# Second expert layer with relu outputs as stationary operand, 256 rows per expert, and a changed order of gathers and table loads

## The chip, the cores and the metric

The kernel runs on one core of a Trainium2 chip. The time of a run is the device time of that core in microseconds; the kernel before was timed three times. One further execution was recorded by the hardware profiler, and all rows shown come from it. Differences of about 0.5% are the least that a measurement of this kernel can tell.

## The reference, cut to what matters

Three stages follow one another: an attention block with heads mixed before and after the softmax, a gated dense feed-forward block, and a mixture of eight experts in which each token goes to one expert. Only the last is changed:

```python
# x: (1792, 768), the dense block's output; w1: (8, 768, 1024); w2: (8, 1024, 768)
logits = x @ w_gate
expert_idx = np.argmax(logits, axis=1)
gate_w = softmax(logits)[np.arange(N), expert_idx]
for e in range(8):
    mask = expert_idx == e
    h = np.maximum(x[mask] @ w1[e], 0.0)
    out[mask] = gate_w[mask, None] * (h @ w2[e])
```

With the reference's inputs the eight experts get 259, 213, 241, 186, 222, 236, 225 and 210 tokens.

## The kernel before, in words

All is written in `feed_forward` (line 415) with an order of instructions fixed by hand: each engine and SP, which issues the loads, executes its instructions in the order in which the program writes them.

**Precision by three products.** Every operand of a large matmul is split into a rounded high part in a reduced float32 type and the low part that is left. `mm3` (line 472) adds three matmuls: high weight by high data (L473), low weight by high data (L474), high weight by low data (L475). The weight tile is the stationary operand, 128 by 128; the data streams past it, 448 columns in the dense layers (the 1792 tokens in four parts `u`) and `CAP` = 264 columns in the experts.

**Weights.** A list `src` names all weight tiles in order: 72 uses for the dense layers (k = 0 to 71), then for each expert four tiles of w1 and four of w2 (k = 72 to 135), 768 KB each. `take` (line 463) hands out the next and looks ahead: it loads up to i+3 on SP (L438, buffer `wraw`, three of them), splits i+2 and loads i+4. `split` (line 440) casts the high part on ScalarE (`whi`, L447) and subtracts for the low part (`wlo`, L451) on GpSimd, or on VectorE where k is in `LOW_W` (line 46: every third k).

**Routing.** `route(u)` (line 577) is a generator in four pieces: the one-hot choice `oh`; slots by prefix sums on TensorE; the list of tokens of the first expert (L609, L610, table `TB0`); then the gate weights and four scatters on GpSimd's queue of (token, gate) pairs into a DRAM table `tab` (L628). The tokens themselves are turned into rows (`turn_row`, `take_row`, `put_row`) and stored in DRAM as `x2`. For the last part, u = 3, this stands between the dense layers and the experts, with `warm` matmuls on constants in between (lines 768 to 796). Then three loads on SP fetch the table for all experts into `TB` (L793); they wait for all table scatters. TB holds 88 rows by 3 per expert.

**Experts.** `fetch(e)` (line 635) issues three indirect loads of 88 rows each from `x2` on GpSimd's queue (L640). `gather(e)` (line 643) transposes them on TensorE (L648; per piece of 128 features three transposes of 88 rows), ScalarE casts the high part (`xhi`), VectorE subtracts the low (`xlo`). The loop at line 831 runs for each expert eight groups `f` of the first layer, 18 matmuls each, with relu on ScalarE (`hhi`) and the low part on VectorE (`hlo`), into PSUM tiles `mm` of which there are five. After group 3 (5 for expert 0) it calls `fetch(e + 1)`. The second layer computes six groups `c` of 24 matmuls, 128 output features by 264 tokens, with the w2 tile stationary; ScalarE copies each group out of PSUM (L864), and after some of them pieces of `gather(e + 1)` run on TensorE (`GATHER`, two after each of the first two groups, one after each of the next two). The result has features on partitions, so `put` (line 799) transposes it back on TensorE (L807, six pieces of three), scales by the gate on VectorE or ScalarE (L814, L812) and scatters three times 88 rows to the output (L816). Three of its pieces run in the second layer (`PARTS`), three in the next expert's first layer.

**Behind the experts.** `blocks` (line 820) counts how many blocks of 128 tokens overflow `CAP`; `overflow` (line 872) computes these in a loop. With at most 264 tokens per expert it does not run.

## Time and profile before

| | |
|---|---|
| three runs | 1424.41, 1429.89, 1430.99 us; median 1429.89 |
| profiled execution, its own time | 1431.59 us |
| its span | 1429.7 us |
| TensorE (PE) busy | 1357.1 us, 95% |
| TensorE weight loads (PEld) | 1179.4 us, 82% |
| VectorE (DVE), ScalarE (ACT), GpSimd (POOL) busy | 57%, 48%, 45% |
| mean granted TensorE clock | 0.981 of 2.4 GHz |
| from HBM, to HBM | 222.46 MB, 45.94 MB |

Attention and the dense layers take the first 1056 us or so, the experts run from 1078 us. Matmuls are pipelined: the duration shown of one is longer than the distance from its start to the next one's, and only the distances add up to time. A wait row says who waited, what came last, the total, how often and the longest.

### The profile page before, as it was taken

How to read it: one execution, taken by the hardware profiler on the slowest of the kernel's cores; microseconds unless marked ns; L12 is line 12 of the kernel's file. 1: busy time of each engine (PE TensorE's matmuls, PEld its weight loads, DVE VectorE, ACT ScalarE, POOL GpSimd, SP SyncE). 2: the span in 40 equal slices, each digit the busy share in tenths (PEclk: the TensorE clock that was granted, in tenths of full speed). 3: DMA queues.
4: the chain of work that ended last, by engine and by line, in shares of the span. 5: the costliest groups of instructions: out<-in, count | busy, mean ns of one | idle time of the engine just before them, and what ended most of it. 6: DMA issues, size and time to landing. Idle time of an engine off the chain costs nothing.

```text
span 1429.7 us, 24918 instructions
## 1 busy us (share of the span) xinstructions
PE 1357.1 (95%) x9144; PEld 1179.4 (82%) x9144; DVE 810.1 (57%) x1562; ACT 690.2 (48%) x1325; POOL 636.4 (45%) x589
## 2 busy tenths in 40 slices
PE   8999999999999999999999999999997899999995
PEld 3677776776777789999999999999977899999995
DVE  3677777766767746606991798189623232433331
ACT  4676666766665533434333433344223354454441
POOL 4676567557654454441112112211035366665662
PEclk9999999999999999999999999999998899999998
DMA  7887787787787687686647765776523466656550
GB/s 243 243 259 236 224 261 243 225 256 245 217 250 213 208 276 269 232 317 214 238 178 263 247 216 188 255 250 213 194 87 125 137 196 205 206 194 203 171 197 21
DMA packets 117060, 307.88 MB, mean 215 GB/s; under 512 B 29198, under 2 KB 72302, under 8 KB 116817
## 3 DMA queue, kind: packets, MB, share of 16 engines
q1 hardware_dynamic: 112577, 294.17, 63.5%
q0 software_dynamic: 4352, 12.02, 3.0%
q8 instruction: 75, 1.23, 0.4%
q14 instruction: 56, 0.46, 0.1%
HBM read 222.46 MB, written 45.94 MB: 188 GB/s over the span
## 4 chain that ended last, share of the span: by engine, by line
PE 74%; DMA 10%; issue 5%; POOL 5%; ACT 2%; SPq 2%; DVE 1%; POOLq 0%; ACTq 0%; DVEq 0%
PE mm L473 16%; PE mm L475 16%; PE mm L474 16%; PE pso L274 8%; PE psm L246 7%; PE psv L302 4%; PE psq L233 4%; DMA qraw<-in_qt 2%; DMA row<-x,TB 2%; POOL wlo L451 2%; DMA xm<-S 2%; DMA wraw<-in_w 2%; POOL row L640 1%; SPq L241 1%; PE tp L648 1%
## 5 line engine op out<-in xcount | busy, mean ns | idle before, releaser
L473 PE MATMUL mm<-xhi,whi 128*128 128x448 f32 (+1 forms) x960 | 326.8, 340 | 1.4 <-ACT xhi L492 1.4
L475 PE MATMUL mm<-xlo,whi 128*128 128x448 f32 (+1 forms) x960 | 322.6, 336 | 0.9 <-POOL xlo L493 0.9
L474 PE MATMUL mm<-xhi,wlo 128*128 128x448 f32 (+1 forms) x960 | 321.8, 335 | 0.0
L451 POOL TENSOR_TENSOR wlo<-wraw,whi 128x1536 fp32r<-128x1536 f32 x54 | 189.3, 3508 | 135.8 <-ACT whi L447 135.0
L474 PE MATMUL mm<-hhi,wlo 128*128 128x264 f32 (+1 forms) x672 | 216.9, 323 | 4.3 <-POOL wlo L451 4.3
L473 PE MATMUL mm<-hhi,whi 128*128 128x264 f32 (+1 forms) x672 | 220.5, 328 | 0.0
L475 PE MATMUL mm<-hlo,whi 128*128 128x264 f32 (+1 forms) x672 | 216.4, 322 | 0.0
L274 PEld LDWEIGHTS pso<-kk,e 120*112 120x112 f32 x1440 | 170.8, 177 | 49.7 <-POOL kk L266 14.8
L447 ACT CAST whi<-wraw 128x1536 fp32r<-128x1536 f32 x136 | 200.9, 1478 | 8.0 <-DMA wraw<-in_w 7.1
L681 DVE RECIPROCAL e<-e 128x448 f32<-128x448 f32 x48 | 141.7, 2952 | 97.8 <-ACT e L680 97.8
L274 PE MATMUL pso<-kk,e 120*112 120x120 f32 x1440 | 180.6, 268 | 16.5 <-ACT AT L282 6.8
L475 PEld LDWEIGHTS mm<-xlo,whi 128*128 128x128 f32 x960 | 181.8, 189 | 13.1 <-POOL xlo L493 2.4
L473 PEld LDWEIGHTS mm<-xhi,whi 128*128 128x128 f32 x960 | 182.0, 190 | 12.1 <-ACT xhi L492 1.7
L474 PEld LDWEIGHTS mm<-xhi,wlo 128*128 128x128 f32 x960 | 182.1, 190 | 10.1
L689 POOL TENSOR_TENSOR hlo<-e,hhi 128x448 fp32r<-128x448 f32 x48 | 57.2, 1191 | 292.5 <-ACT hhi L688 292.5
L246 PE MATMUL psm<-xm,K 120*120 120x448 f32 x360 | 169.8, 554 | 5.6 <-DMA xm<-S 5.4
L266 POOL TENSOR_SCALAR kk<-K,r 120x120 f32<-120x120 f32 x180 | 108.5, 603 | 144.2 <-DVE r L263 114.2
L254 ACT ACTIVATE e<-psm,nm 120x448 f32<-120x448 f32 x180 | 115.5, 642 | 96.1 <-DVE r L263 94.3
L474 PEld LDWEIGHTS mm<-hhi,wlo 128*128 128x128 f32 x672 | 128.5, 191 | 10.2 <-POOL wlo L451 5.0
L473 PEld LDWEIGHTS mm<-hhi,whi 128*128 128x128 f32 x672 | 128.6, 191 | 5.0
L475 PEld LDWEIGHTS mm<-hlo,whi 128*128 128x128 f32 x672 | 128.4, 191 | 5.3
L688 ACT CAST hhi<-e 128x448 fp32r<-128x448 f32 x48 | 27.3, 568 | 213.9 <-DVE e L683 213.9
(127 smaller groups left out, 2082.7 us busy)
## 6 DMA issues: line engine op xcount, KB each, us to landing
wraw<-wf SPq DMA_DIRECT2D x72, 768.0 KB
wraw<-in_w SPq DMA_DIRECT2D x64, 768.0 KB
wlo<-wl SPq DMA_DIRECT2D x54, 768.0 KB
xm<-S SPq DMA_DIRECT2D x360, 105.0 KB
f<-in_wx SPq DMA_DIRECT2D x72, 384.0 KB
wf<-cva SPq DMA_DIRECT2D x72, 192.0 KB
wl<-wlo SPq DMA_DIRECT2D x18, 768.0 KB
qraw<-in_qt SPq DMA_DIRECT2D x56, 180.0 KB
```

The source lines that it names most:

```text
L233: nc.tensor.matmul(ps[:m, :S], QS[t, h // 3][i][:, h % 3, :m], k, start=(i == 0), stop=(i == 1))
L246: nc.tensor.matmul(ps[:, :S], K1, XS.pop(n), start=True, stop=True)
L254: nc.scalar.activation(e, ps[:, :S], AF.Exp, bias=nm, scale=1.0, accum_out=su)
L266: nc.gpsimd.tensor_scalar(out=kk, in0=K2, scalar1=r2, scalar2=1.0, op0=ALU.mult, op1=ALU.mult)
L274: nc.tensor.matmul(po[:, c, :120], e[:, 112 * c:112 * c + 112], kk, start=True, stop=True)
L447: A.copy(a, r)
L451: (V if k in LOW_W else G).tensor_tensor(out=b, in0=r, in1=a.bitcast(F32), op=ALU.subtract)
L473: nc.tensor.matmul(ps, w[0][:, j, :], x[0], start=first, stop=False)
L474: nc.tensor.matmul(ps, w[1][:, j, :], x[0], start=False, stop=False)
L475: nc.tensor.matmul(ps, w[0][:, j, :], x[1], start=False, stop=last)
L681: V.reciprocal(out=e, in_=e)
L689: G.tensor_tensor(out=hl, in0=e, in1=hh.bitcast(F32), op=ALU.subtract)
```

## The change

For experts 1 to 7 the second layer is turned round: the relu outputs (128 hidden features by 128 tokens) become the stationary operand and w2, stored with hidden features on partitions and all 768 outputs in the free dimension, streams past them in halves of 384 columns. The four sums (two halves of tokens by two halves of outputs) are held in four PSUM tiles through all eight hidden groups and come out as token rows, so that one scaling copy each (ScalarE for the first half of the outputs, VectorE for the second) and two scatters of 128 rows finish the expert. These experts hold 256 tokens in two tiles of 128; expert 0 keeps 264 tokens in three of 88 and the old second layer. `fetch(e + 1)` follows the first group in place of the fourth (expert 0: still the sixth); one gather piece follows each hidden group but the first. The table is loaded by five loads after the third group of expert 0; the rest of `route(3)` stands ahead of `warm(6)` and `gather(0)`; all four last row halves are turned in one go, two of them through `mm` buffers. From k = 72 on every second `wlo` goes to VectorE.

```diff
-CAP = 264
-TS = CAP // 3
+CAP = [264] + [256] * 7
+TS = CAP[0] // 3
...
-LOW_W = {0} | {k for k in range(200) if k % 3 == 2 and not 18 < k < 72}
+LOW_W = {0} | {k for k in range(200) if (k % 3 == 2 and k < 18) or (k % 2 == 0 and k >= 72)}
...
         def fetch(e):
             RG[e] = []
-            for t in range(3):
-                r = ro.tile([112, DM], F32, name="row")
+            n = 128 if e else TS
+            for t in range(2 if e else 3):
+                r = ro.tile([128, DM], F32, name="row")
...
         def gather(e):
             XE[e] = []
+            n = 128 if e else TS
             for c in range(6):
...
-                for t in range(3):
-                    nc.tensor.transpose(p[:, t * TS:t * TS + TS], RG[e][t][:TS, 128 * c:128 * c + 128], ID[:TS, :TS])
+                for t, r in enumerate(RG[e]):
+                    nc.tensor.transpose(p[:, t * n:t * n + n], r[:n, 128 * c:128 * c + 128], ID[:n, :n])
...
-        for j in (0, 1):
-            turn_row(3, j, 1)
-        for j in (0, 1):
+        for j in range(4):
+            turn_row(3, j, 1, pm if j > 1 else None)
+        for j in range(4):
             take_row(3, j, 1)
             put_row(3, j, 384, DM)
-        warm(1)
         next(go)
-        for j in (2, 3):
-            turn_row(3, j, 1)
-        for j in (2, 3):
-            take_row(3, j, 1)
-            put_row(3, j, 384, DM)
-        warm(2)
+        warm(3)
         next(go)
         fetch(0)
+        for _ in go:
+            pass
         warm(6)
         for _ in gather(0):
             pass
-        for _ in go:
-            pass
-        for t in range(3):
-            ld = nc.sync.dma_start(out=TB[:, :, t, :], in_=tab.rearrange("(e s) t -> s e t", e=NE)[t * TS:t * TS + TS])
...
+        def put(e, acc):
+            for t in range(2):
+                row = RT[:, (2 * e + 1 + t) % NE, :]
+                g = TB[:, e, t, 1:2].bitcast(F32)
+                A.activation(row[:, :384], acc[t][0][:, :384], AF.Copy, scale=g)
+                V.tensor_scalar(out=row[:, 384:], in0=acc[t][1][:, :384], scalar1=g, scalar2=None, op0=ALU.mult)
+                sc = G.indirect_dma_start(out=out, out_offset=bass.IndirectOffsetOnAxis(ap=TB[:, e, t, 0:1], axis=0), in_=row, in_offset=None, bounds_check=NT - 1, oob_is_err=False)
+                apart("out", sc)
...
                 hs.append((hh, hl))
+                if e == 0 and f == 2:
+                    for t in range(5):
+                        o, i = (TBF[:, t, :], tab[t * TS:t * TS + TS]) if t < 3 else (TB[:, 1:, t - 3, :], tab.rearrange("(e s) t -> s e t", e=NE)[128 * (t - 3):128 * (t - 2), 1:])
+                        ld = nc.sync.dma_start(out=o, in_=i)
+                        for sc in routed:
+                            tc.add_manual_dep(from_inst=ld.ins, to_name=sc.ins.name, info=mybir.DependencyInfo(mybir.DependencyClass.Sync, mybir.DependencyReason.DATA))
+                if f == (5 if e == 0 else 0) and e + 1 < NE:
+                    fetch(e + 1)
                 next(done, None)
-                if e == 0 and f == 3:
+                if e == 0 and f == 6:
                     blocks()
-                if f == (5 if e == 0 else 3) and e + 1 < NE:
-                    fetch(e + 1)
...
+            acc = [[pm.tile([128, 512], F32, name="mm") for hf in range(2)] for t in range(2)]
+            for f in range(8):
+                if f % 2 == 0:
+                    w = [z.rearrange("p a b -> p (a b)") for z in take()]
+                for t in range(2):
+                    for hf in range(2):
+                        o = f % 2 * DM + 384 * hf
+                        h = [z[:, 128 * t:128 * t + 128] for z in hs[f]]
+                        ps = acc[t][hf][:, :384]
+                        nc.tensor.matmul(ps, h[0], w[0][:, o:o + 384], start=(f == 0), stop=False)
+                        nc.tensor.matmul(ps, h[0], w[1][:, o:o + 384], start=False, stop=False)
+                        nc.tensor.matmul(ps, h[1], w[0][:, o:o + 384], start=False, stop=(f == 7))
+                if f > 0:
+                    next(parts, None)
+            put(e, acc)
```

The weight layout on the host and the overflow loop are adapted to the new form of w2; for expert 0 the old second layer and its `put`, now `put0` with its own table `TBF`, are kept.

## Rows read from the trace of the kernel before

**Rows 1.** Stretches: us, busy (instructions) PE, PEld, DVE, ACT, POOL; PE clock; DMA share; GB/s.

```profile
1056.00:1078.12 22.12, 16.64 (x89) 10.85 (x87) 4.73 (x17) 3.46 (x9) 6.83 (x11) 0.87 0.25 69
1078.12:1097.82 19.70, 19.70 (x149) 19.70 (x148) 6.12 (x20) 6.99 (x12) 8.70 (x10) 0.89 0.34 105
1097.82:1133.48 35.66, 23.74 (x174) 22.89 (x172) 9.30 (x13) 12.06 (x21) 17.87 (x7) 0.81 0.47 143
1133.48:1411.29 277.81, 271.04 (x2251) 269.59 (x2249) 94.04 (x138) 130.31 (x202) 168.53 (x96) 0.99 0.58 184
```

**Rows 2.** The same view, experts 1 to 7 (fastest, last, sum of all seven).

```profile
1252.51:1290.97 38.46, 38.46 (x327) 38.38 (x325) 14.67 (x21) 19.28 (x31) 23.74 (x14) 1.00 0.64 205
...
1374.65:1413.53 38.88, 38.62 (x318) 37.75 (x315) 10.30 (x16) 15.43 (x24) 17.57 (x11) 1.00 0.30 100
sum 280.05, PE 273.02 PEld 270.70 DVE 95.18 ACT 131.17 POOL 168.81; mean PE 39.00 PEld 38.67 DVE 13.60 ACT 18.74 POOL 24.12
```

**Rows 3.** Timeline of TensorE, expert 4's second layer: start us, us, line, operation.

```profile
1281.37 0.28 PE L475 MATMUL mm<-hlo,whi 128*128 128x264 f32 x1
...
1283.89 0.28 PE L475 MATMUL mm<-hlo,whi 128*128 128x264 f32 x1
1284.01 0.49 PE L807 MATMUL tp<-CS,x2T 128*88 128x128 f32 x3
1284.34 0.39 PE L648 MATMUL tp<-CS,row 88*128 88x88 f32 x3
1284.52 0.37 PE L473 MATMUL mm<-hhi,whi 128*128 128x264 f32 x1
```

**Rows 4.** Timeline of TensorE in a dense layer.

```profile
900.00 0.37 PE L473 MATMUL mm<-hhi,whi 128*128 128x448 f32 x1
...
904.13 0.36 PE L475 MATMUL mm<-hlo,whi 128*128 128x448 f32 x1
```

**Rows 5.** Waits, 1055 to 1135 us: who, for what, us in total, times, longest.

```profile
PE tp L648 <- DMA row<-x,TB: 13.5, 6, 5.3
...
ACT whi L447 <- DMA wraw<-in_w: 6.5, 1, 6.5
```

**Rows 6.** Waits of SP's queue, 1055 to 1430 us.

```profile
SPq L793 <- DMA tab<-en,si: 25.7, 1, 25.7
```

**Rows 7.** Timeline of SP's queue, the table loads.

```profile
1089.51 1.75 SPq L793 DMA_DIRECT2D TB<-tab  x3
```

**Rows 8.** Chain of work that ended last, three links: start us, us, what.

```profile
1069.74 4.48 DMA row<-x,TB
...
1085.51 3.88 DMA tab<-en,si
...
1188.02 8.38 DMA row<-x,TB
```

**Rows 9.** Timelines of TensorE, VectorE and GpSimd at the end of the last expert.

```profile
1411.29 0.94 PE L807 MATMUL tp<-CS,x2T 128*88 128x128 f32 x6
...
1413.57 0.61 DVE L814 TENSOR_SCALAR WT<-tp,TB 88x384 f32<-88x384 f32 x1 [0.62 <-PE tp L807]
...
1415.85 0.99 POOL L816 DMA_INDIRECT out<-WT,TB  x1 [0.21 <-issue]
```

**Rows 10.** Waits of TensorE, 1133 to 1411 us.

```profile
PE tp L648 <- DMA row<-x,TB: 5.4, 5, 2.3
PE mm L474 <- POOL wlo L451: 1.4, 2, 0.7
```

**Rows 11.** VectorE's wlo subtractions: ns min/median/max from 1078; mean ns from 1133 us.

```profile
L451 DVE TENSOR_TENSOR wlo<-wraw,whi x21: 1757/1759/4934, 1081.4 to 1395.2; 128x1536 fp32r<-128x1536 f32 x21
...
L451 DVE TENSOR_TENSOR wlo<-wraw,whi 128x1536 fp32r<-128x1536 f32 x18 | 40.9, 2271 | 18.2 <-ACT whi L447 16.3 <-issue 1.9
```

**Rows 12.** Timeline of TensorE in attention, plain float32 and the next.

```profile
402.06 1.01 PE L246 MATMUL psm<-xm,K 120*120 120x448 f32 x2
402.56 0.71 PE L233 MATMUL psq<-ks,qhi 128*110 128x448 f32 x1
```

More of the change, by code (lines that the diff above doesn't have):

```diff
@@ L507, in feed_forward @@
         load(3)
-        WT = cst.tile([112, NE, DM], F32, name="WT")
+        WT = cst.tile([128, NE, DM], F32, name="WT")[:112]
         WG = cst.tile([128, 6, NE], F32, name="WG")
@@ L551, in feed_forward, with turn_row @@
         X2T, ROW, HALF, LG, routed, late = {}, {}, {}, {}, [], []
-        def turn_row(u, j, hf):
-            t = HALF[u, j, hf] = pt.tile([128, 3, 128], F32, name="tp")
+        def turn_row(u, j, hf, where=None):
+            t = HALF[u, j, hf] = where.tile([128, 512], F32, name="mm")[:, :384].rearrange("p (a b) -> p a b", b=128) if where else pt.tile([128, 3, 128], F32, name="tp")
             for i in range(3):
@@ L559, in take_row @@
             if (u, j) not in ROW:
-                ROW[u, j] = ro.tile([112, DM], F32, name="row")
-            (eng or A.copy)(ROW[u, j][:, 384 * hf:384 * hf + 384], HALF.pop((u, j, hf))[:112].rearrange("p i c -> p (i c)"))
+                ROW[u, j] = ro.tile([128, DM], F32, name="row")
+            (eng or A.copy)(ROW[u, j][:112, 384 * hf:384 * hf + 384], HALF.pop((u, j, hf))[:112].rearrange("p i c -> p (i c)"))
         def put_row(u, j, lo=0, hi=DM):
-            nc.sync.dma_start(out=x2[u * U + 112 * j:u * U + 112 * j + 112, lo:hi], in_=ROW[u, j][:, lo:hi])
+            nc.sync.dma_start(out=x2[u * U + 112 * j:u * U + 112 * j + 112, lo:hi], in_=ROW[u, j][:112, lo:hi])
         def logit(u, n):
@@ L600, in route @@
             V.tensor_reduce(out=sf, in_=sl, axis=AX.X, op=ALU.add)
-            eqs = [sm.tile([112, CAP], F16, name="at", bufs=4) for j in range(4)]
+            eqs = [sm.tile([112, CAP[0]], F16, name="at", bufs=4) for j in range(4)]
             for j in range(4):
@@ L851, in feed_forward @@
             parts = gather(e + 1) if e + 1 < NE else iter(())
[L852 to L866 removed]
+            if e == 0:
+                y = []
+                done = put0(y)
+                for c in range(6):
+                    ps = pm.tile([128, 512], F32, name="mm")[:, :CAP[0]]
+                    for f in range(8):
+                        j = c * 8 + f
+                        if j % 12 == 0:
+                            w = take()
+                        mm3(ps, w, j % 12, hs[f], f == 0, f == 7)
+                        if (c, f) in PARTS:
+                            next(done)
+                    t = yp.tile([128, U], F32, name="x2T")[:, :CAP[0]]
+                    A.copy(t, ps)
+                    y.append(t)
+                    for _ in range(GATHER[c]):
+                        next(parts, None)
+                continue
+            acc = [[pm.tile([128, 512], F32, name="mm") for hf in range(2)] for t in range(2)]
+            for f in range(8):
+                if f % 2 == 0:
[9 more added lines that the diff above has]
+                if f > 0:
                     next(parts, None)
[L868 to L869 removed]
+            put(e, acc)
 def overflow(tc, w1, w2, out, x2, tab, keep):
@@ L886, in overflow @@
                     t = rb.tile([128, 2], I32, name="ot")
-                    nc.sync.dma_start(out=t, in_=tab[bass.ds(i * 128 + (e * STR + CAP), 128), :])
+                    nc.sync.dma_start(out=t, in_=tab[bass.ds(i * 128 + (e * STR + CAP[e]), 128), :])
                     r = rb.tile([128, DM], F32, name="orow")
@@ L906, in overflow @@
                         p = pm.tile([128, 128], F32, name="om")
+                        w = wp.tile([128, 12, 128], F32, name="ow")
                         for f in range(8):
-                            j = c * 8 + f
-                            if j % 12 == 0:
-                                w = wp.tile([128, 12, 128], F32, name="ow")
-                                nc.sync.dma_start(out=w, in_=w2[e, j // 12])
-                            nc.tensor.matmul(p, w[:, j % 12, :], h[:, f, :], start=(f == 0), stop=(f == 7))
+                            i = w2[e, (c * 8 + f) // 12, :, (c * 8 + f) % 12] if e == 0 else w2[e, f // 2, :, f % 2 * 6 + c]
+                            nc.sync.dma_start(out=w[:, f, :], in_=i)
+                        for f in range(8):
+                            nc.tensor.matmul(p, w[:, f, :], h[:, f, :], start=(f == 0), stop=(f == 7))
                         y = yb.tile([128, 128], F32, name="oy")
```

61 lines of the change are left out of this document (21 added, 40 removed).

## The prediction, made before the changed kernel ran

> **What bounds the kernel now.** I first cut the span into stretches by what TensorE does [rows 1]. The experts begin at 1078.12 us and hold the last 351 us. In the first row, the hand-over from the dense layers, TensorE waits for routing. In the next two, the first expert, it is busy for 43.44 of 55.36 us. In the fourth, the other seven experts, for 271.04 of 277.81: there the stream of matmuls is the bound, and the DMA engines are only 0.58 busy. Then I cut that fourth stretch into experts [rows 2]. The fastest takes 38.46 us with TensorE busy throughout; the sum over all seven rows is 280.05 us, so the six before the last take 280.05 - 38.88 = 241.17 us, 10.4 more than six times the fastest.
>
> A busy TensorE says little about its pace, so I read starts from the timeline [rows 3]: from 1281.37 to 1283.89 there are 21 starts of 264 columns, 120 ns each. Three transposes of expert results hold the engine from 1284.01 to 1284.34 (0.33 us), three of gathered rows until 1284.52 (0.18 us). In the fastest expert 288 matmuls at 120 ns are 34.56 us; the other 3.90 us are twelve such interruptions, six of each kind, 0.325 us each with the restart behind them. The dense layers have 448 columns: 20 starts from 900.00 to 904.13 are 206.5 ns each [rows 4].
>
> In the first expert TensorE waits for the next expert's rows and ScalarE waits 6.5 us for weights [rows 5]. The cause stands in SP's queue: the table load L793 waited 25.7 us for the table scatters [rows 6], and its three loads left at 1089.51 [rows 7]. Weight loads are queued behind them on SP. The chain shows the links: the last scatter was issued at 1085.51 and took 3.88 us to land, and rows fetched beside weight loads took 8.38 us to arrive (issued at 1188.02), against 4.48 us at 1069.74 with little else moving [rows 8].
>
> **Times.** The sum goes against the profiled execution, 1431.59 us, which has 1.9 us around its span of 1429.7; the median is 1429.89, 0.1% lower.
>
> **Second layer, experts 1 to 7.** Per expert 144 matmuls of 264 columns become 96 of 384. No expert matmul of 384 exists, so I interpolate between the rows on either side: 120 + (384 - 264) x (206.5 - 120)/184 = 176.4 ns. Bounds: 384 columns at the 2.4 GHz that the granted clock of 1.00 stands for are 160 ns; at the 448-column rate they are 177 ns. I take 176.4: 96 of them are 16.93 us, where 144 x 120 ns were 17.28. The trace's spacing exceeds columns over 2.4 GHz by 10 ns at 264 and 20 ns at 448. The Trainium skill, "TensorE: Matmul & The Clock Gate", section "Back-to-back issue gap", gives columns/2.4 plus 2.5 ns for an isolated matmul; at 384 that would be 162.5 ns, and the seven experts together 9 us less than mine. The trace disagrees with it at both widths.
>
> The six groups of result transposes go (6 x 0.325 = 1.95 us), with them six ScalarE copies out of PSUM and three scatters, replaced by four copies of 384 columns and two scatters. Those lie beside matmuls, and ScalarE and VectorE are busy for 130.31 and 94.04 of 277.81 us [rows 1]. The results now hold four of five PSUM buffers until these copies; the next expert's first group uses the fifth, and its second comes about 2.1 us later, while a copy of 384 columns takes 0.61 us at the tail [rows 9]. I cost that at nothing. If VectorE is held by a long subtraction, its first result buffer is wanted again at the next expert's third group, about 4 us on.
>
> **256 columns.** The same line gives 116.2 ns for 256 columns, so 144 are 16.74 us, 0.54 less per expert. Bounds: 0 (the stream is not set by columns) and 0.54. Six gathers transpose two times 128 columns in place of three times 88; I leave them at 0.325 us each (two transposes at a third of 0.33 and the restart are 0.30).
>
> So a steady expert takes 16.74 + 16.93 + 1.95 = 35.62 us, 2.84 less than 38.46: **17.0 us** for experts 1 to 6. The last expert, with no gather, takes 33.67 us where its matmuls ran from 1374.65 to 1411.29 [rows 2, 9], 36.64 us: **3.0**. Two groups of expert 0's result transposes remain in expert 1's stretch: **-0.65**.
>
> **Fetch earlier, subtractions moved.** Inside experts 1 to 7 TensorE's named waits are for fetched rows (5.4 us) and for wlo (1.4 us); low clock behind these gaps and the waits of its weight loads make up the rest of the 10.4 [rows 1, 10]. Issuing the fetch at the first group in place of the fourth puts it three groups of 18 matmuls, some 6.3 us, earlier, with about 15 us until the gather: more than the 8.38 us that a landing took. On POOL it stands behind only two scatters of the previous expert, and no longer behind a subtraction. Half of the wlo subtractions, not a third, now go to VectorE, which takes 2.27 us on the mean [rows 11]. I take 9.0 of the 10.4 us back; bounds 0 and 10.4: **9.0**.
>
> **First expert.** Its floor is 19.70 us (first layer, with its slow start) plus 17.28 plus ten interruptions of 0.325, 40.2; 55.36 were spent, so 15.2 were lost. After the change the rest of the routing is issued ahead of the gather. Its small VectorE operations fall where VectorE idles; POOL issues the four scatters right behind fetch(0), so by about 1076, landed by 1079. The five table loads stand on SP behind a weight load that waits for its buffer until about 1083 (VectorE's first expert subtraction begins at 1081.4 and takes 1.76 us [rows 11]), and find the scatters landed. Behind them on SP are weight loads only, now held by some 3 us of issuing, not by a wait. Weight loads 76 and 77 go ahead of them, so the second layer finds its first tile. Fetch(1), still at the sixth group, is issued around 1090 and its rows are there around 1100, when the first of its transposes is due. I take 14 of 15.2; bounds 6 and 15.2: **14.0**.
>
> **Hand-over.** Four row halves are now transposed, copied and stored in one go, two through pm buffers: the last store leaves up to 0.7 us earlier, and the routing matmuls stand behind six more transposes, which end while VectorE still makes oh. Against it, a weight load that stood behind the table loads now runs beside fetch(0): its landing could go from 4.48 towards 8.38 us. Bounds: 0.7 gain, 4 loss; I take **0**, since store and load leave before the fetch.
>
> **Tail.** The last scatter was issued 4.56 us after the last matmul [rows 9]. Now a copy of about 0.6 us and two issues of 1.3 us follow, the first of them begun before the matmuls end: about 1 us. **3.5**, bounds 2 and 4.
>
> Sum: 17.0 + 3.0 - 0.65 + 9.0 + 14.0 + 0 + 3.5 = 45.85, and 1431.59 - 45.85 = 1385.7, so **1386 us**.
>
> **Rivals.**
> (a) The first expert stays starved, because the table or fetch(1) is late again: 6 of 14 us come back, 1394 us. For it: rows land slowly beside weights [rows 8]. Chance 0.12.
> (b) The link is the bound. The fastest expert moved 205 GB/s over 38.46 us, 7.9 MB [rows 2]; in 35.62 us that is 221 GB/s. If 205 were the ceiling, the 17 us would not come: 1403 us. Against it: the share is 0.64 there. Chance 0.08.
> (c) VectorE and GpSimd block each other. One VectorE subtraction took 4.93 us, the mean is 2.27 [rows 11]; each of 28 such late ones could cost TensorE 0.7 us, one of the two wlo waits [rows 10], 20 us, and the copies behind them more: 1406 to 1411 us. Against it: casts come over 4 us apart, and they now alternate between the engines. Chance 0.08. The Trainium skill, "SBUF — State Buffer", section "Who interferes with whom", says that a VectorE instruction with two SBUF inputs and a GpSimd one that reads SBUF exclude each other; the row of 4.93 us agrees, and the rule speaks against moving work to VectorE.
> (d) The spacing hardly grows with columns, so 384 costs 120 ns: 96 x 56 ns x 7 = 38 us more, 1348 us. The same page on TensorE, same section of the Trainium skill, lists sustained spacings of 81 ns at 128 columns and 131 ns at 512. The 206.5 ns at 448 is against it [rows 4]. Chance 0.02.
> (e) Slower than before: nothing in this trace has the reduced float32 type below 264 columns. If 256 lay below an edge where it falls to the rate of plain float32, two instructions of 448 columns from 402.06 to 402.56 [rows 12], 1.12 ns a column, a first-layer matmul would take 286 ns: 1008 x 170 ns = 171 us, 1557 us. It decides at about 45 us, a third of that. For it is only that both widths seen are above 256; the 120 and 206.5 ns lie nearly on one line through zero, with no sign of an edge. Chance 0.02.
> (f) The change does not do what it says if an expert overflows 256 rows and takes the loop behind. Computing the reference's routing gives 259 tokens for expert 0 and at most 241 for others. Below 0.01.
>
> **How the numbers follow.** The forecast has 0.63, the rest (0.05) is mixtures. Its own range is 1375 (160 ns at 384: 11 us less) to 1393. The upper end takes in (a) and (b) and most of (c): 1408. Differences under 0.5% a measurement of this kernel cannot tell from none. Only (e), and a stall that I do not see, end slower: 0.04; 0.02 is left for the same.
>
> **What would show it.** Right: starts 0.176 us apart in second layers and 0.116 in first ones; stretches near 35.6 us; no wait of SP for tab; no wait of TensorE for fetched rows; last scatter about 1 us behind the last matmul. Wrong: stretches still above 38 us, an idle stretch in the first expert, or spacing off the line.

## The result and the profile after

The changed kernel takes 1374.65 us (median of four, 1374.53 to 1375.61), the kernel before 1427.15 us (median of four, 1421.01 to 1430.99): ratio 0.9638, 95% interval 0.9598 to 0.9677. The forecast was 1386 us with a range of 1375 to 1408: the sign and the mechanisms held, and the time lies 0.35 us below the range. The profiled execution after took 1375.61 us, with a span of 1373.8 us.

The stretches of [rows 1] after the change, in the same columns, with the tail as a fifth:

```profile
1053.00:1075.77 22.77, 15.88 (x85) 10.17 (x83) 5.79 (x25) 3.59 (x10) 10.25 (x17) 0.87 0.38 102
1075.77:1095.25 19.48, 19.48 (x148) 19.48 (x148) 8.57 (x15) 8.85 (x13) 8.94 (x4) 0.89 0.51 163
1095.25:1114.80 19.55, 19.55 (x168) 19.55 (x166) 7.63 (x11) 10.03 (x18) 8.65 (x4) 1.00 0.47 163
1114.80:1361.60 246.80, 246.80 (x1764) 245.41 (x1761) 94.49 (x135) 117.60 (x162) 126.45 (x69) 1.00 0.61 206
1361.60:1373.80 12.20, 0.16 (x1) 0.00 (x0) 0.62 (x1) 0.26 (x1) 2.14 (x4) 0.70 0.16 59
```

From the first expert matmul to the last, TensorE is now busy in all 285.83 us; in [rows 1] it stood idle for 11.9 us of the second layer of expert 0 and for 6.8 of the other seven experts. Single experts, against [rows 2] (expert 4, the last, the sum of experts 1 to 7):

```profile
1221.76:1257.07 35.31, 35.31 (x254) 35.11 (x254) 13.95 (x20) 17.43 (x25) 18.86 (x11) 1.00 0.63 218
...
1327.69:1361.60 33.91, 33.91 (x241) 33.75 (x240) 9.74 (x13) 12.43 (x17) 14.72 (x8) 1.00 0.35 115
sum 246.80, PE 246.80 PEld 245.41 DVE 94.49 ACT 117.60 POOL 126.45; mean PE 35.26 PEld 35.06 DVE 13.50 ACT 16.80 POOL 18.06
```

TensorE's timeline, answering [rows 3]: starts of expert 4's second layer, one gather piece in it, and starts of expert 5's first layer.

```profile
1250.87 0.34 PE L887 MATMUL mm<-whi,hhi 128*128 128x384 f32 x1
...
1252.25 0.34 PE L889 MATMUL mm<-whi,hlo 128*128 128x384 f32 x1
1252.43 0.38 PE L652 MATMUL tp<-CS,row 128*128 128x128 f32 x2
1252.56 0.42 PE L887 MATMUL mm<-whi,hhi 128*128 128x384 f32 x1
1252.82 0.33 PE L888 MATMUL mm<-wlo,hhi 128*128 128x384 f32 x1
...
1257.18 0.28 PE L475 MATMUL mm<-xhi,wlo 128*128 128x256 f32 x1
...
1259.33 0.28 PE L475 MATMUL mm<-xhi,wlo 128*128 128x256 f32 x1
```

Eight steps from 1250.87 to 1252.25 are 172.5 ns each; eighteen from 1257.18 to 1259.33 are 119.4 ns. Without the gather piece the second start behind 1252.25 would stand at 1252.60; it stands at 1252.82, so the piece with its two transposes costs 0.22 us.

All waits of TensorE from 1050 to 1370 us, against [rows 5] and [rows 10]:

```profile
PE tp L652 <- DMA row<-x,TB: 5.9, 3, 3.5
PE tp L652 <- issue: 0.5, 1, 0.5
PE tp L652 <- DVE xlo L656: 0.5, 1, 0.5
```

They all belong to the hand-over: from 1076 us on there is none. SP's queue, against [rows 7]; its wait for the table scatters [rows 6] is gone:

```profile
1057.15 2.06 SPq L565 DMA_DIRECT2D x<-row  x4
1059.30 20.70 SPq L439 DMA_DIRECT2D wraw<-in_w  x2
1080.32 1.10 SPq L848 DMA_DIRECT2D TBF<-tab  x3
1081.46 1.01 SPq L848 DMA_DIRECT2D TB<-tab  x2
```

GpSimd's timeline: the first fetch of expert 0, of expert 1, and the last two scatters, against [rows 9]:

```profile
1064.67 1.02 POOL L643 DMA_INDIRECT row<-x,TB  x1 [8.04 <-issue]
...
1087.74 0.99 POOL L643 DMA_INDIRECT row<-x,TB  x1 [0.15 <-issue]
...
1362.15 1.00 POOL L818 DMA_INDIRECT out<-WT,TB  x1 [10.08 <-ACT WT L816]
...
1363.46 0.98 POOL L818 DMA_INDIRECT out<-WT,TB  x1 [0.22 <-issue]
```

And the `wlo` subtractions of [rows 11], in ns (min/median/max):

```profile
L452 DVE TENSOR_TENSOR wlo<-wraw,whi x31: 1757/1759/1760, 1077.9 to 1346.9; 128x1536 fp32r<-128x1536 f32 x31
L452 POOL TENSOR_TENSOR wlo<-wraw,whi x31: 3485/3512/3707, 1084.1 to 1348.4; 128x1536 fp32r<-128x1536 f32 x31
```

### The profile page after: what moved, and what is told of

The parts are those of the page before. It is cut to its first block, busy times and chain, and to the rows that moved or that the text cites. A ratio compares the mean times of both kernels' runs of the same rounds, so it can differ in the third digit from the quotient of the medians.

```text
span 1373.8 us, 23768 instructions
## 1 busy us (share of the span) xinstructions
PE 1327.1 (97%) x8640; PEld 1152.8 (84%) x8640; DVE 817.4 (59%) x1559; ACT 676.4 (49%) x1283; POOL 584.9 (43%) x557
## 4 chain that ended last, share of the span: by engine, by line
PE 86%; DMA 5%; DVE 2%; issue 2%; ACT 2%; POOL 1%; SPq 1%; POOLq 0%; ACTq 0%
PE mm L474 17%; PE mm L476 17%; PE mm L475 17%; PE pso L275 9%; PE psm L247 7%; PE psv L303 5%; PE psq L234 4%; PE mm L887 3%; PE mm L888 3%; PE mm L889 3%; DMA xm<-S 2%; DMA qraw<-in_qt 1%; PE tp L652 1%; ACT e L255 1%; PE tp L557 1%
## 5 line engine op out<-in xcount | busy, mean ns | idle before, releaser
L474 PE MATMUL mm<-xhi,whi 128*128 128x448 f32 (+2 forms) x960 | 324.9, 338 | 1.3 <-ACT xhi L493 1.3
L476 PE MATMUL mm<-xlo,whi 128*128 128x448 f32 (+2 forms) x960 | 322.5, 336 | 1.1 <-POOL xlo L494 1.0
L475 PE MATMUL mm<-xhi,wlo 128*128 128x448 f32 (+2 forms) x960 | 322.0, 335 | 0.0
L452 POOL TENSOR_TENSOR wlo<-wraw,whi 128x1536 fp32r<-128x1536 f32 x43 | 151.1, 3513 | 166.6 <-ACT whi L448 166.2
L475 PEld LDWEIGHTS mm<-xhi,wlo 128*128 128x128 f32 x960 | 183.1, 191 | 10.2
L572 DVE CUSTOM_DVE_ANT_0 junk<-row,WT 112x768 f32<-112x768 f32 x96 | 121.0, 1260 | 2.2
L474 PE MATMUL mm<-hhi,whi 128*128 128x448 f32 (+1 forms) x336 | 120.7, 359 | 0.0
L475 PE MATMUL mm<-hhi,wlo 128*128 128x448 f32 (+1 forms) x336 | 119.3, 355 | 0.0
L476 PE MATMUL mm<-hlo,whi 128*128 128x448 f32 (+1 forms) x336 | 118.3, 352 | 0.0
L452 DVE TENSOR_TENSOR wlo<-wraw,whi 128x1536 fp32r<-128x1536 f32 x39 | 69.6, 1786 | 76.9 <-ACT whi L448 72.8
L252 DVE TENSOR_REDUCE nm<-psm 120x1 f32<-120x448 f32 x180 | 110.2, 612 | 3.6 <-PE psm L247 3.6
```

What stands on the lines that cost most here:

```text
L252: nc.vector.tensor_reduce(out=nm, in_=ps[:, :S], axis=AX.X, op=ALU.max, negate=True)
L452: (V if k in LOW_W else G).tensor_tensor(out=b, in0=r, in1=a.bitcast(F32), op=ALU.subtract)
L474: nc.tensor.matmul(ps, w[0][:, j, :], x[0], start=first, stop=False)
L475: nc.tensor.matmul(ps, w[1][:, j, :], x[0], start=False, stop=False)
L476: nc.tensor.matmul(ps, w[0][:, j, :], x[1], start=False, stop=last)
L572: V.tensor_tensor_reduce(out=jk, in0=ROW[u, j][:112], in1=WT[:, e, :], scale=1.0, scalar=0.0, op0=ALU.mult, op1=ALU.add, accum_out=LG[u][: ...
```

## The experiments

Every run below is read by five stages, cut at starts in TensorE's timeline (us): from the last group of the dense layers' gate matmuls to the first expert matmul (hand-over); expert 0; experts 1 to 6; the last expert to the start of its last matmul; from there to the end of the span (tail). What lies ahead is nearly the same code in every kernel (some tile sizes and the engine of one `wlo` subtraction differ), yet its end falls between 1050.6 and 1059.1 us over fourteen profiles; the stages leave that out. The run is the median of four (best: five); before_fetch_first, before_low_half, widths and three_scatters were run once. Each stands beside runs of the kernel before on the same chip (medians 1426.06 to 1427.30). The stages are of one profile each. The kernels after, widths and three_scatters have the same code up to expert 1 and differ by 0.98 us in the hand-over and 0.36 us in expert 0, so smaller differences there tell nothing.

| kernel | hand-over | expert 0 | 1 to 6 | last | tail | sum | run, us |
|---|---|---|---|---|---|---|---|
| before | 19.01 | 55.36 | 241.17 | 36.51 | 18.54 | 370.59 | 1427.15 |
| after | 20.49 | 39.03 | 212.89 | 33.73 | 12.38 | 318.52 | 1374.65 |
| layer_only | 19.12 | 52.92 | 212.89 | 33.73 | 12.36 | 331.02 | 1387.90 |
| order_only | 19.69 | 40.92 | 230.16 | 36.52 | 18.52 | 345.81 | 1402.51 |
| before_fetch_first | 19.02 | 56.36 | 232.28 | 36.52 | 18.12 | 362.30 | 1417.38 |
| before_low_half | 20.37 | 45.72 | 240.72 | 36.53 | 17.04 | 360.38 | 1421.67 |
| tab_old_place | 18.39 | 38.70 | 212.89 | 33.74 | 12.32 | 316.04 | 1372.34 |
| go_late | 20.62 | 41.37 | 212.90 | 33.73 | 12.16 | 320.78 | 1375.06 |
| tab_and_go_old | 19.46 | 43.53 | 212.89 | 33.74 | 12.19 | 321.81 | 1378.79 |
| low_thirds | 19.94 | 40.69 | 212.92 | 33.73 | 11.86 | 319.14 | 1375.13 |
| load_late | 18.73 | 39.54 | 212.93 | 33.73 | 12.06 | 316.99 | 1373.16 |
| widths | 19.64 | 39.21 | 257.71 | 33.74 | 12.04 | 362.34 | 1419.37 |
| three_scatters | 19.51 | 38.85 | 212.89 | 33.74 | 13.26 | 318.25 | 1375.42 |
| best | 18.62 | 38.43 | 212.90 | 33.73 | 11.65 | 315.33 | 1372.82 |

### The layer alone and the order alone

layer_only is the kernel after with the old order of routing, table loads, fetches and subtractions:

```diff
-LOW_W = {0} | {k for k in range(200) if (k % 3 == 2 and k < 18) or (k % 2 == 0 and k >= 72)}
+LOW_W = {0} | {k for k in range(200) if k % 3 == 2 and not 18 < k < 72}
...
+        for _ in go:
+            pass
+        for t in range(5):
...
-                if f == (5 if e == 0 else 0) and e + 1 < NE:
-                    fetch(e + 1)
...
+                if f == (5 if e == 0 else 3) and e + 1 < NE:
+                    fetch(e + 1)
```

> The changed kernel with the whole old order: row halves turned in two pairs, rest of the routing behind gather(0), table loads ahead of the expert loop, fetch after the fourth group, every third wlo on VectorE. Theory A (the two halves of the change add up; the order is worth the first expert's 16 us and the 10 us of stalls of the others, less 1.5 us at the hand-over): 25 us over the changed kernel, about 1400 us, first expert near 54 us, experts 1 to 6 near 37 us on the mean with waits for fetched rows. Theory B (with two fetches, two scatters and no result transposes GpSimd is free enough that the stalls of experts 1 to 7 go without the new order): first expert alone slow, experts 1 to 6 at 35.3 us, about 1390 us.

order_only is the kernel before with the reverse of that diff (three table loads in place of five) and with the row halves turned in one go.

> The kernel before, with 264 columns, three tiles of 88 and the old second layer, and only the new order (row halves in one go, routing ahead of the gather, table loads behind the third group, fetch after the first group, every second wlo on VectorE). Theory A: the first expert falls from 55 to about 39 us and experts 1 to 6 run at the fastest one's 38.5 us: 25 us under the kernel before, about 1402 us. Theory B (the stalls come from three scatters and three fetches on GpSimd): only the first expert gains, about 1412 us.

Ratios to the kernel before: 0.9725 (0.9693 to 0.9758) and 0.983 (0.9795 to 0.9864). The layer alone brings 38.7 us (1426.61 - 1387.90), the order alone 24.1, together 62.8 where both at once bring 52.5. The table shows why: experts 1 to 6 fall to 212.89 us with the layer alone, to the figure of the kernel after, and the order alone brings them to 6 x 38.36, about the pace of the fastest expert of before. So either half removes the 10.4 us of stalls, and they are counted twice. Theory A of layer_only fell with this, and its B held; A of order_only held. How the layer removes the stalls stands in the timelines of GpSimd and TensorE. The gather does not come later: its first piece begins 21.4 us into experts 2 to 6 in layer_only and 21.6 to 22.4 us in the kernel before. The rows come earlier: the last fetch is issued 10.0 to 11.9 us into these experts, where it was 14.1 to 16.1. Two fetches stand there in place of three, and the two scatters are issued by 2.6 us, where the last of three came at 10.2 to 11.6. Which of the two counts more was not run.

Expert 0, on the other hand, needs the order: 52.92 us without it. SP's queue of layer_only has the old picture, first as a wait, then in the timeline:

```profile
SPq L798 <- DMA tab<-en,si: 25.8, 1, 25.8
```

```profile
1081.94 1.09 SPq L798 DMA_DIRECT2D TBF<-tab  x3
1083.08 1.02 SPq L798 DMA_DIRECT2D TB<-tab  x2
1084.20 2.12 SPq L439 DMA_DIRECT2D wraw<-in_w  x3
```

Three weight loads leave only behind the table.

### Which part of the order removes the stalls of experts 1 to 6

before_fetch_first is the kernel before with the fetch at the first group (`f == (5 if e == 0 else 0)`) and nothing else. before_low_half is the kernel before with the new `LOW_W` and nothing else.

> The kernel before, with fetch(e + 1) after the first group from expert 1 on and nothing else. Theory A (the rows are late because the fetch is issued late): no TensorE wait for fetched rows in experts 1 to 6, their sum falls from 241.2 to 231 to 234 us. Theory B (they are late because GpSimd's subtractions stand ahead of the fetch): the sum stays above 237 us.

> The kernel before, with every second wlo of the experts on VectorE in place of every third and nothing else. Theory A: the waits for wlo go, the waits for rows stay, the sum of experts 1 to 6 falls by 2 to 4 us from 241.2. Theory B: with less on GpSimd the fetch too is earlier, the sum falls to 231 to 234 us.

The fetch alone brings 8.9 of the 10.4 us (241.17 - 232.28): theory A held, and TensorE waits for no rows in experts 1 to 6; two waits for `wlo`, 1.7 us, are left. The subtractions alone bring 0.45 us: the waits for `wlo` go and those for rows stay (6.9 us), as theory A had it, but its 2 to 4 us did not come, and theory B fell. On top of the earlier fetch they bring more: order_only, with both, has 230.16 us, 2.1 less than the fetch alone, and no wait of TensorE in these experts. And the subtractions took 9.6 us off expert 0, which neither theory had. GpSimd's timeline shows how. In the kernel before, the first fetch of expert 1 stands behind a subtraction that waits for a weight tile held up on SP:

```profile
1097.55 3.44 POOL L451 TENSOR_TENSOR wlo<-wraw,whi 128x1536 fp32r<-128x1536 f32 x1 [7.47 <-ACT whi L447]
1101.18 2.33 POOL L640 DMA_INDIRECT row<-x,TB  x1 [0.19 <-issue]
```

In before_low_half that subtraction is on VectorE, and the fetch waits for the table instead:

```profile
1094.00 1.02 POOL L640 DMA_INDIRECT row<-x,TB  x1 [2.73 <-DMA TB<-tab]
```

So the table loads do their harm along a chain of two queues: table scatters, SP, weight load, cast, GpSimd's subtraction, fetch, transposes. Moving the subtraction that stands ahead of the fetch cuts the chain in the middle.

### Which part of the order feeds expert 0

tab_old_place puts the five table loads back between `gather(0)` and the experts; go_late puts only the rest of `route(3)` back behind `gather(0)`; tab_and_go_old does both; low_thirds puts back only the old `LOW_W`. The first:

```diff
         for _ in gather(0):
             pass
+        for t in range(5):
...
-                if e == 0 and f == 2:
-                    for t in range(5):
```

> The changed kernel with the five table loads ahead of the expert loop again, so ahead of weight load 76 on SP; the scatters stay ahead of the gather. Theory A (what starved the first expert was that the scatters came late, not where the loads stand): the scatters have landed by about 1077, load 76 starts near 1079 and is in time, the first expert stays near 39 us, and the hand-over loses its contention as in load_late: 1373 to 1375 us. Theory B (the place decides): first expert 46 us or more, 1382 us or more.

> The changed kernel with the rest of the routing (gate weights and scatters) behind gather(0) again; the table loads stay behind the third group. Theory A: the scatters land near 1088, SP holds only load 78 and later ones for that long, which had to wait for a buffer until 1087.6 anyway; fetch(1) comes about 3 us later; first expert 39 to 42 us, 1375 to 1378 us. Theory B (the early scatters carry the gain): first expert 46 us or more, 1382 us or more.

> The changed kernel with both the scatters behind gather(0) and the table loads ahead of the expert loop, as in the kernel before; wlo still half on VectorE. Theory A (either move alone keeps SP from holding weight load 76, so only both undone starve the first expert; of the 16 us some 10 hang on which engine subtracts): first expert near 45 us, as with the old order and half of wlo on VectorE alone (45.7), 1380 to 1382 us. Theory B (the two moves carry all 14 to 16 us): first expert 53 us or more, 1388 us or more.

> The changed kernel with only every third wlo of the experts on VectorE again. Theory A (the engine of the subtractions matters only while weights arrive late): first expert 39 to 40 us, experts 1 to 6 unchanged at 212.9 us, 1374 to 1376 us. Theory B (VectorE's larger share carries part of the gain by itself): first expert 42 us or more, or waits for wlo in the others, 1378 us or more.

Expert 0 takes 38.70, 41.37, 43.53 and 40.69 us, against 39.03 in the kernel after. All four lie nearer to their theory A than to B; A was missed by tab_and_go_old, which was to take 45 us here and 1380 to 1382 in all, and by low_thirds, 39 to 40 us here. The early scatters alone suffice: with them the table loads can stand in their old place, for the scatters were issued by 1067.16 and SP issued the loads from 1070.86. With late scatters the table loads' later place limits the loss to 2.3 us. Both undone cost 4.5 us, not 15, since the subtractions still keep GpSimd free; there the fetch of expert 1 waited for the table:

```profile
1091.15 0.99 POOL L643 DMA_INDIRECT row<-x,TB  x1 [4.48 <-DMA TB<-tab]
```

It was issued 3.4 us later than in the kernel after (1087.74) in a kernel whose stages began at nearly the same time (1055.29 against 1055.28). The subtractions alone are worth 1.7 us of expert 0 once the weights are in time. So the parts cover for one another: each is worth little while the others stand.

### What the move of the table loads costs

In the kernel after, the hand-over is 1.48 us longer than before. A weight load (k = 76) now leaves SP at 1059.30, right behind the row stores, where the table loads used to hold it. load_late holds that load until the fetch of expert 0 has landed, and changes nothing else:

```diff
-                nc.sync.dma_start(out=rawt[k], in_=src[k])
+                ld = nc.sync.dma_start(out=rawt[k], in_=src[k])
+                if k == 76:
+                    for sc in FETCHED:
+                        tc.add_manual_dep(from_inst=ld.ins, to_name=sc.ins.name, info=mybir.DependencyInfo(mybir.DependencyClass.Sync, mybir.DependencyReason.DATA))
```

> The changed kernel, with weight load 76 held on SP until the three rows of fetch(0) have landed. Theory A (the hand-over grew because this load now runs beside the last row stores, for whose landing fetch(0) waits): fetch(0) is issued about 8.0 us after the last gate matmuls begin instead of 9.4, the experts begin 1.5 us earlier, about 1373 us. Theory B (fetch(0) waits for the routing itself): no change, 1374.7 us. Theory C (the load is then too late for its use in the first expert's second layer): 1376 us or more.

1373.16 us (1369.33 to 1374.42), ratio 0.9612 (0.9576 to 0.9648), which by its interval is not settled against the 0.9638 of the kernel after; the experts begin 1.76 us sooner after the gate matmuls, near theory A's 1.5. GpSimd's timeline of load_late:

```profile
1062.70 1.02 POOL L647 DMA_INDIRECT row<-x,TB  x1 [6.23 <-DVE en L631]
```

Its last gate group began at 1055.11, so the fetch leaves 7.6 us behind it, where the kernel after has 1064.67 - 1055.28 = 9.4 us. The fetch reads what the row stores write, and by the DMA packets of the traces their last packet ends 7.75 us behind the gate group in the kernel after and 5.88 in load_late, 1.6 and 1.7 us ahead of the fetch.

The pair makes the load look dearer than it is. three_scatters and widths, with the load as free as in the kernel after, issue the fetch 8.1 and 8.6 us behind the gate group, and before_low_half and tab_and_go_old, with the load held, 9.35 and 8.5. The mean of the six profiles with the load free is 8.8 us, that of the eight with it held 8.0. In hand-overs, the six with the load free have 19.51 to 20.62 us, three with the new order and the load held 18.39 to 18.73 (tab_old_place, load_late, best): about 1.4 us between the means. tab_and_go_old, held too but with the rest of the routing behind the gather, has 19.46 against the 20.62 of go_late. So a free load costs about 1 us there. That it does so by delaying the stores is shown in the pair and not over all: in four of the six the last store packet is as early as in load_late, 5.5 to 6.0 us, and the fetch follows 2.6 to 3.1 us behind it, so that part of the wait stays open. The old order with the load held gives 19.01 to 20.37, 19.4 on the mean, so the new order of routing gains up to 0.8 us there, and the freed load takes it back.

### The width of the moving data

widths cuts the 256 columns of the first layer in two for three experts: 128 and 128, 192 and 64, 224 and 32. The work is the same, in twice as many matmuls.

```diff
-                for c in range(6):
-                    mm3(ps, w, f % 2 * 6 + c, XE[e][c], c == 0, c == 5)
+                cuts = {2: (0, 128, 256), 3: (0, 192, 256), 5: (0, 224, 256)}.get(e, (0, CAP[e]))
+                for lo, hi in zip(cuts, cuts[1:]):
+                    for c in range(6):
+                        mm3(ps[:, lo:hi], w, f % 2 * 6 + c, [z[:, lo:hi] for z in XE[e][c]], c == 0, c == 5)
```

> The changed kernel, with the first layer's matmuls cut into two column ranges in three experts: 128 and 128 in expert 2, 192 and 64 in expert 3, 224 and 32 in expert 5; the others as before. It measures what one matmul of the reduced float32 type costs at these widths. Theory A (the stream goes by columns, 0.45 to 0.47 ns each): starts 59 ns apart at 128, 89 at 192, 104 at 224, the three experts as long as the others. Theory B (a floor of about 120 ns under 256 columns, as 264 and 256 columns both stand at 120): 120 ns at each width, and 17 us more in each of the three experts. Theory C (an edge below 256 where the type falls to the rate of plain float32, 1.12 ns a column): 143 ns at 128, 214 at 192, 250 at 224, 72 at 64.

First layers of experts 2, 3, 4 (uncut) and 5, in the columns of [rows 1]:

```profile
1150.38:1182.48 32.10, 32.10 (x289) 32.10 (x289) 7.11 (x10) 8.39 (x12) 12.84 (x9) 1.00 0.46 159
1200.60:1232.67 32.07, 32.07 (x289) 32.07 (x289) 7.10 (x10) 8.39 (x12) 12.85 (x9) 1.00 0.47 161
1250.85:1268.11 17.26, 17.26 (x145) 17.26 (x145) 6.94 (x10) 8.41 (x12) 11.76 (x9) 1.00 0.77 261
1286.16:1318.23 32.07, 32.07 (x289) 32.07 (x289) 7.11 (x10) 8.39 (x12) 12.85 (x9) 1.00 0.46 160
```

Where the cuts lie makes no difference: 288 matmuls at 111.4 ns in each case. TensorE's timeline, first and last of fifteen steps at 192 columns and of ten at 32:

```profile
1204.82 0.27 PE L476 MATMUL mm<-xlo,whi 128*128 128x192 f32 x1
...
1206.50 0.27 PE L476 MATMUL mm<-xlo,whi 128*128 128x192 f32 x1
...
1288.87 0.26 PE L475 MATMUL mm<-xhi,wlo 128*128 128x32 f32 x1
...
1289.98 0.26 PE L476 MATMUL mm<-xlo,whi 128*128 128x32 f32 x1
```

That is 112 and 111 ns. There is a floor of about 111 ns to a reduced float32 matmul with a weight load of its own, and theory B came near, with the floor where it had the 120 ns of [rows 3] and 14.9 us more in each of the three experts where it had 17. Theory A fell. So did C: at 128, 192 and 224 columns the rate of plain float32 would have given 143, 214 and 250 ns; at 32 and 64 it would lie under the floor and could not be told.

### The tail

The span ends 10.34 us behind the last scatter's issue, where the kernel before took 13.85 (1429.7 - 1415.85). Is it the count of scatters, two for three? three_scatters issues a third behind the last two, of eight rows into the row buffer of the dense block, and so writes eight rows more than the kernel after:

```diff
+            if e == NE - 1:
+                G.indirect_dma_start(out=x2, out_offset=bass.IndirectOffsetOnAxis(ap=TB[:8, e, t, 0:1], axis=0), in_=row[:8, :], in_offset=None)
```

> The changed kernel with one more scatter behind the last expert's two: eight rows to a scratch tensor. In the eleven profiles so far the span ended 12.4 to 13.9 us after the start of the last scatter's issue where three scatters of 88 rows came last, 9.8 to 10.3 where two of 128 did. Theory A (the number of scatters in flight sets that time): 12.4 to 13.9 us behind the third, so the tail grows by 3.5 to 5 us. Theory B (the rows in flight or the form of 88 rows set it): at most 10.3 us behind the third, the tail grows by the 1.3 us of an issue at most.

```profile
1362.37 0.98 POOL L818 DMA_INDIRECT out<-WT,TB  x1 [0.23 <-issue]
1363.34 0.09 POOL L479 MEMSET gap<- 1x1 f32 x1
1363.66 0.89 POOL L821 DMA_INDIRECT x<-WT,TB  x1 [0.23 <-issue]
```

The span ends at 1373.6, 9.94 us behind the third. The count of scatters in flight is not the cause: theory A fell, and B held with a tail longer by 0.88 us. The four kernels with three scatters of 88 rows end 12.35 to 13.85 us behind the last issue, those with two of 128 rows 9.83 to 10.34.

A part of the difference stands at the end of GpSimd's program, behind the landing. Its last line in before, after and three_scatters, in ns (min/median/max):

```profile
L947 POOLq DRAIN  x3: 46/106/5299, 1423.6 to 1429.4; - x3
L970 POOLq DRAIN  x3: 46/107/4156, 1368.8 to 1373.5; - x3
L972 POOLq DRAIN  x3: 46/107/4237, 1368.5 to 1373.3; - x3
```

In each of the three kernels the span ends about 0.84 us behind the longest of the three. A semaphore instruction ahead of it (INC_SWDGE_SEM) takes 1468, 1188 and 1208 ns. The three programs issue 64, 50 and 51 indirect transfers on GpSimd's queue. Fourteen fewer make the two instructions shorter by 1143 and 280 ns, one more makes them longer by 81 and 20: about 0.1 us at the end for each such transfer, for those left out between the experts and for the one added behind them alike. That is 1.4 of the 3.5 us. By the DMA packets of the traces another 1.4 is the landing: the last packet on that queue ends 4.94 us behind the last issue before and 3.57 after. Whether the rows or their number make that landing shorter, and what the last 0.7 us are, stays open.

### The table loads in their old place and the last expert's second layer split

best takes the table loads in their old place (which holds load 76), runs the last expert's second layer one tile of tokens after the other so that its first scatter leaves early, and moves the last subtraction to VectorE:

```diff
+            if e == NE - 1:
+                ws = []
+                for t in range(2):
+                    for f in range(8):
+                        if t == 0 and f % 2 == 0:
+                            ws.append([z.rearrange("p a b -> p (a b)") for z in take()])
...
+                    put(e, acc, (t,))
+                continue
```

> The changed kernel with the table loads ahead of the expert loop (as in tab_old_place) and, in the last expert, the second layer's two token halves one after the other, so that the first half's copies and scatter lie beside the second half's matmuls; the last wlo goes to VectorE. Theory A: hand-over and first expert as in tab_old_place (18.4 and 38.7 us), one scatter less behind the last matmul: 12.3 us of tail become 9.5 to 11, 1370 to 1372 us. Theory B (the last weight tiles are then needed twice as fast and arrive late): TensorE waits in the last second layer, 2 us or more, and nothing is won.

The last expert stayed fed (33.73 us), so theory B fell. Theory A held for the hand-over and expert 0 (18.62 and 38.43 us), not for the tail (11.65 us, where it had 9.5 to 11), and the run misses its 1370 to 1372 us by 0.8. TensorE over its matmuls, then the two scatters:

```profile
1327.22:1361.10 33.88, 33.88 (x241) 33.74 (x240) 11.41 (x14) 12.41 (x17) 12.09 (x9) 1.00 0.37 127
```

```profile
1354.40 1.00 POOL L823 DMA_INDIRECT out<-WT,TB  x1 [8.69 <-DVE WT L822]
...
1362.72 0.98 POOL L823 DMA_INDIRECT out<-WT,TB  x1 [7.23 <-DVE WT L822]
```

The stages add up to 3.2 us less than in the kernel after: 1.87 at the hand-over, 0.60 in expert 0, 0.73 in the tail. Of the 1.87 about one may be the spread of the hand-over that was told above. 1372.82 us (1370.87 to 1374.51), ratio 0.9618 (0.9604 to 0.9633), lies 1.8 us under the median of the kernel after, but the intervals overlap: by the trace it is a little faster, by the runs not settled. tab_old_place, without the split, has 1372.34 us and 0.9621, so the runs show nothing that the split adds.

## Why the prediction was right, and where it was short

The stages fell by 370.59 - 318.52 = 52.1 us, where the terms add up to 45.85. Another 3.8 us of the profiled pair lie ahead of the change: the profile that I summed against had the latest begin of the hand-over among fourteen, 1059.11 us, and the kernel after began it at 1055.28. The last 1.0 us is the profiled execution (1375.61) against the median. 6.2 + 3.8 + 1.0 are the 11 us between 1385.7 and 1374.65, so over a third of the miss was in no term at all: one profiled execution was taken as the baseline, though the three runs already spread by 6.6 us.

- **Steady expert: right, 35.31 for 35.62.** The second layer was close: 173.3 ns for 384 columns (16.64 us of 96), where the line gave 176.4. Two errors beside it cancelled. The first layer takes 17.27 us, not 16.74: at 256 columns the line from 264 downward gave 116.2 ns, and 119.9 was measured on the mean, close above the floor of 111. So the narrowing to 256 columns brought nearly nothing. And a gather piece of two transposes costs about 0.23 us (six are the 1.40 us that remain of 35.31), not 0.325. A group of three result transposes still costs 0.33 (expert 1 below). That is 0.11 to 0.12 us a transpose, near the floor of the matmuls, and leaves next to nothing for the "restart" that I had reckoned with.
- **Experts 1 to 6: short by 2.9.** The forecast was 17.0 + 9.0 - 0.65 = 25.35, measured 28.28: six times 3.15 (38.46 - 35.31) is 18.9, all 10.4 us of stalls went, and expert 1 took 36.32, a loss of 1.0. I had put two groups of expert 0's result transposes there; there are three, at 1117.03, 1119.51 and 1121.98 us. That the time of the stalls is won back by an earlier fetch held (before_fetch_first), but the layer alone would have won it too. The subtractions, which I named beside the fetch, brought 0.45 us alone and 2.1 on top of it.
- **Last expert: right,** 2.78 for 3.0.
- **First expert: right in its cause, short by 2.3.** 16.33 us for 14, beyond the upper bound of 15.2: the floor of 40.2 us had ten interruptions at 0.325. There are nine, three of result transposes and six gather pieces; with 0.33 and 0.23 us the floor is 39.35, and 39.03 was measured. The chain through SP was read rightly as far as the weights; that it runs on through GpSimd's queue, where the fetch stands behind the subtraction of a late tile, is in GpSimd's timeline of before, and I did not look there. It is why the subtractions alone brought 9.6 of the 16.3 us, and why with them either the early scatters or the late table loads were nearly enough.
- **Hand-over: 1.48 us lost, forecast 0, inside the bounds.** (With the 19.51 and 19.64 of three_scatters and widths the loss is 0.5 to 1.5.) "Store and load leave before the fetch" was the wrong half of the step. The weight load did not slow the fetched rows, which still took 4.45 us by the chain of the kernel after; it made the fetch itself later, in the pair with load_late by later stores:

```profile
1067.31 4.45 DMA row<-x,TB
```

- **Tail: by its ratio the term most mis-sized, 6.16 for 3.5, beyond the upper bound of 4.** The last issue comes 2.04 us behind the start of the last matmul, where it was 4.69: 2.65 us, where I had reckoned the whole 3.5. What I left out is the time from that issue to the end, 10.34 for 13.85: I had taken it as fixed, and 1.4 us of it go with the number of indirect transfers.

**The rivals.** (a) is out: TensorE waits for no rows in expert 0. (b) is out: 218 to 223 GB/s flow in experts 1 to 6, above the 205 that would have been the ceiling. (c) is out: all 31 VectorE subtractions take 1.76 us. With a third of the subtractions on VectorE single ones reach 3.16 (layer_only) and 3.88 us (low_thirds); with every second one there they take 1.76 in before_low_half, order_only and the kernel after. In the kernel before, each of the five VectorE subtractions of over 3 us begins while one of GpSimd's runs, the longest so:

```profile
1229.21 3.49 POOL L451 TENSOR_TENSOR wlo<-wraw,whi 128x1536 fp32r<-128x1536 f32 x1
1229.39 4.93 DVE L451 TENSOR_TENSOR wlo<-wraw,whi 128x1536 fp32r<-128x1536 f32 x1 [0.93 <-issue]
```

In the kernel after none does. So alternating the engines removed the collisions that it was suspected of. The Trainium skill, "SBUF — State Buffer", section "Who interferes with whom", which stood behind that rival, is not contradicted by this: the two kinds of instruction simply no longer met, but for 0.34 us at 1348.36, where VectorE's had begun first. (d) is out with 173 ns at 384 columns, (e) with 119.4 ns at 256 and 111 to 112 at 224, 192 and 128.

The Trainium skill, "TensorE: Matmul & The Clock Gate", section "Back-to-back issue gap", would give 162.5 ns at 384 columns; the trace has 173, so that sum, 9 us lower, would have fallen nearer to the result for a reason that does not hold.

## What to carry to other kernels

Follow a late transfer through every queue that it passes: here a table load on one queue delayed a fetch on another by way of a weight load and a subtraction, and cutting that chain in its middle brought back 9.6 of 16.3 us. Measure the halves of a change each by itself before crediting them, since two parts can remove the same stall, and profile a kernel more than once before a difference of a microsecond is explained; and take the baseline of a sum stage by stage, not from the end of one execution. Before narrowing a tile, check that its instruction is still priced by its columns.

## What the runs showed of the hardware that was not expected

- Reduced float32 matmuls with a weight load each start 111 to 112 ns apart from 32 to 224 columns, 119.4 at 256, 172.5 at 384 and, before, 206.5 at 448. The Trainium skill, "TensorE: Matmul & The Clock Gate", section "LDWEIGHTS (loading the stationary operand)", has a weight load take its columns over 1.2 GHz; for 128 columns that is 107 ns, near the floor. No run here varied the stationary columns, so that the load sets the floor is not shown.
- With a weight load issued right behind small stores, what waits for the stores was issued 0.8 us later on the mean of the profiles (8.8 and 8.0 us behind the gate group; 1.8 in one pair), and the gathers of rows behind it stayed at 4.45 us.
- GpSimd's closing DRAIN took 5299, 4237 and 4156 ns in programs with 64, 51 and 50 indirect transfers on its queue, and the INC_SWDGE_SEM ahead of it 1468, 1208 and 1188: about 0.1 us at the end for each transfer of the program.
